# Attention block on one core: set-up rebuilt, two value buffers, two GpSimd chains and another plan

## The chip, the cores and the metric

One core of a Trainium2 chip runs the kernel. The metric is the device time in microseconds (us) of one execution, the median of several; lower is better. The engines are named as in the profile: PE (matrix multiply), ACT (ScalarE), DVE (VectorE), POOL (GpSimd) and SP (which only issues DMAs).

## The reference

```python
B, S, D, H = 1, 2048, 448, 16        # x [1,2048,448], wqkv [448,1344], wo [448,448], bf16
Dh = D // H                          # 28
qkv = (x @ wqkv).reshape(B, S, 3, H, Dh).transpose(2, 0, 3, 1, 4)
q, k, v = qkv
p = softmax(einsum("bhqd,bhkd->bhqk", q, k) * Dh ** -0.5)
return einsum("bhqk,bhkd->bhqd", p, v).transpose(0, 2, 1, 3).reshape(B, S, D) @ wo
```

## The kernel before

**Tiling.** The 16 heads form four groups of four; a group's heads lie in four strips of 32 partitions (28 rows of the head, one row for offsets, three of padding). Queries are cut into four blocks of 512, keys into 16 blocks of 128. A group with a query block is a *window*; there are 16. A window has 16 rows (key blocks) of four score tiles, one for each head, 128 keys by 512 queries; 1024 tiles in all. A tile is one matmul of a strip pair of KB with one of QB (L935), which leaves in PSUM the exponent of the softmax term, scaled so that its upper bits, taken as an integer, are already close to the bits of the bf16 result. The largest key entry of a head (KMAX) times |q| serves as an upper bound that is taken off; it comes in through the other strip of each pair, which holds |q| on the query side and the negative maximum on the key side.

**Three ways to finish a tile.** (1) ACT: two tiles share a double bank PA, and one Exp over 128x1024 (L1364) writes bf16 to a PTA buffer. (2) DVE and POOL: DVE makes DU (L1139) and DV (L1142), POOL multiplies them to DG (L1145), DVE adds DG and writes PTD (L1158); the tile's bank PD (three of them) is held until then. (3) POOL alone ("lone chain", `start_g`): DVE copies the bank to SG (L1071) and frees it, then POOL does six steps on it: GU, GE, GV, GU, SG, PTD (L1078 to L1101). There is one set of GU, GV, GE, so one such chain is in work at a time; `ahead` picks tiles some rows ahead of need.

**After that.** A row of four finished tiles is multiplied with V (VA) into the one bank PO (L1203), which adds up 16 rows; a window's sum goes to OSB, its reciprocal denominators travel through DRAM and come back broadcast as RRB, POOL multiplies (L1038) to OT, and PE multiplies OT with `wo`. The first two windows (NF = 2) first do only their first four rows (FB = 4) each, with a provisional bound from key block 0 alone (KPART[:, 0]); `task_factor` later computes the factor that brings those sums to the final bound.

**Set-up.** x comes in blocks of 512 rows: XS[0] to XS[2] by plain loads on SP and the fourth transposed by DMA (L310). WK is loaded on ACT's queue (L299), WQ behind XS[0] on SP (L306). PE transposes a block in two halves of eight 128x112 pieces (L462) into PSUM; DVE or ACT copies to XT (L473, L475). POOL spreads WK's columns to the 32-row strips (WKP, L425), ACT does the same for WQ (L426). Four matmuls make K of block 0 (L578), four make Q (L714). ACT writes Q twice (QB, L730 and L732), DVE takes absolute values (QP, L738), reduces K to its largest entries (L587, L592), and |q| times that bound goes to the other strips, by DVE (L749) or POOL (L746). ACT copies K with a mask and a bias (`bndcol`, L596 and L599). The maxima of all key blocks (`task_kmax`, L630) become NK, which DMAs replicate into the key strips (L652). Constants are filled by memsets: the unit rows of XT (L359) and V's ones (L360) on DVE, the masks `mcol`, `bdiff`, `selcol`, `bndcol` on POOL (L348 to L356).

**Order.** Nothing is left to a run-time scheduler. At build time the kernel simulates its engines with fixed costs: each `Op` has an engine, a cost, a latency, dependencies, a priority and conditions. `try_pe`, `try_act` and `try_static` pick the next operation whenever an engine is free, and the instructions are issued in the order found. `pos` counts score tiles started. The lists in PLAN hold 16 numbers, one for each window: from which row lone chains are taken (AHEAD), how long POOL holds back for DVE's tiles (GCLEAR), by how much a PE operation may overrun the end of a running exponential (SLK, in `fits`), due times of Q, K, V and so on. Engines run their own queues in order, so an instruction that waits holds everything behind it on that engine. An operation of kind "sb" (fast SBUF-to-SBUF on DVE, L762 and L766) is started only near the end of a POOL instruction.

Of the kernel before, what the change touches and what calls it, by code (L numbers as in the profile page):

```python
# [21 lines left out]
P = 128  # L22
H = 16
HP = 32
G = 4
# [7 lines left out]
KEPS = 1e-6  # L33
# [12 lines left out]
    "PVROWS": [8, 10, 10, 3, 6, 7, 11, 7, 7, -10, 7, 7, 11, 11, 11, 9],  # L46
    "AHEAD": [16, 9, 16, 15, 7, 10, 12, 8, 12, 13, 11, 6, 13, 7, 11, 5],
    "GCLEAR": [0.4, -0.4, -0.3, 0.3, 0.2, 0.7, 0.3, -0.1, 0.2, 1, 0.5, 1, 0.4, 0.8, 1.4, 0.1],
    "SCLEAR": [0, 1.1, 1.8, 1.7, 1.4, 0.4, 0.7, 0, 0.3, 1.5, 0.1, 0.9, 1.8, 2, 0.4, 1.8],
    "LEAD1": [39, 10, 29, 7, 3, 3, 6, 33, 3, 26, -6, 23, -9, -3, 11, 13],  # L50
    "LEAD2": [35, 8, 37, 43, 45, 13, 27, 43, 38, 19, 20, 49, 27, 32, 24, 29],
    "LEAD3": [0.1, 13, 2, 7, 45, 0.1, 8, -6, 5, -9, 24, 2, -2, 27, 12, 1],
    "LEADC": [30, 0, 39, 26, 16, 30, 14, 14, 37, -2, 23, 43, 34, 20, -3, 13],
    "PVMORE": [3, 9, 6, 1, 2, 5, 3, 4, 4, 3, 2, 6, 2, 2, 0, 8],
    "QFROM": [8, 0, 13, -18, 2, -7, -14, -3, -29, 0, 15, -30, 2, 27, 2, 20],
    "QBY": [64, 33, 84, 35, 80, 63, 48, 35, 70, 68, 37, 26, 24, 83, 73, 82],
    "QLEAD": [-88, 27, 38, -61, -3, -56, 48, 32, 6, -83, 0, 17, 28, -85, -90, 11],
    "KFROM": [34, 11, 29, -12, -10, -8, 19, 19, 18, 30, 41, -14, 27, 26, 8, 2],
    "KBY": [23, 12, 48, -4, 29, 50, 40, 54, 30, -2, 2, 49, 14, 48, 9, 40],
    "KLEAD": [34, 27, -74, -63, -7, -50, 32, 24, 1, -25, -43, -62, 18, -27, -8, 47],  # L60
    "VFROM": [-2, 8, 7, 30, -2, 49, 8, 15, 40, -1, -5, 24, 46, -9, 35, 43],
    "VBY": [41, 25, 52, 0, 56, 14, 11, 57, 57, 37, 59, 4, 57, -8, 17, 49],
    "VLEAD": [48, 73, 0, -21, 9, -23, 6, 54, 46, 20, 21, -27, -34, 9, -21, -1],
    "NORM": [20, 10, -10, 38, 6, 40, 20, 10, -14, -4, 9, -10, -18, 20, 32, -1],
    "TAIL": [8, 8, 40, 1],
    "PART": [-34, -19, 34, 37, -30, 40, 3, 30],
    "OUT": [0, 10, 28, 39, 20, -22, 7, -6, 5, -8, -2, 39, -30, -10, 13, 39],
    "SLK": [0.2, 0.22, 0.21, 0.19, 0.12, 0.21, 0.2, 0.12, 0.24, 0.11, 0.08, 0.22, 0.17, 0.19, 0.27, 0.12],
# [6 lines left out]
TDEP = 0.12  # L75
# [12 lines left out]
EVU = 0.598  # L88
DISS = 0.6
# [28 lines left out]
def kernel(  # L118
# [29 lines left out]
    NG = 3  # L148
    GMAX = 1
# [42 lines left out]
    FE2 = 80  # L192
# [3 lines left out]
    TE = 0  # L196
    CPE = 1
    REDP = 0
    TW = 0
    XLAT = (4.6, 7.3, 8.9, 9.6)  # L200
    WQLAT = 5.9
    XSP = 1
    KP0 = -4377
    KP1 = -4375
    KP2 = -4485
    BP2 = 34
    PBND = ((3,), (2, 3))
    VE = 16
    UV = 4
    BW = (-1, 4, 1)  # L210
    THF = (0, 1, 0, 0)
    EVP = (-1200, -4365, -700, 0)
    KEVP = (0, 200, 200, 200)
    WQE = 'ACT'
    QORD = 0
    KCH = ((1, 2), (2, 4))
    RCH = ((1, 4), (0, 1))
    XT3 = 14.0
    XBAR = True
    KENG = ('ACT', 'DVE', 'DVE', 'DVE')  # L220
    HENG = ('ACT', 'DVE', 'DVE', 'DVE')
# [24 lines left out]
    RK0 = sb([P, 1], F32, "RK0")  # L246
# [3 lines left out]
    VA = [sb([P, NKT, HG, HP], BF16, f"VA{g}") for g in range(G)]  # L250
# [8 lines left out]
    GU = sb([P, QW], F16, "GU")  # L259
    GV = sb([P, QW], F16, "GV")  # L260
    GE = sb([P, QW], F32, "GE")
# [24 lines left out]
    maskm = sb([P, QW], BF16, "maskm")  # L286
# [3 lines left out]
    bndcol = [sb([P, 1], F32, f"bndcol{pr}") for pr in range(2)]  # L290
    mcol = sb([P, 1], F32, "mcol")
    bdiff = sb([P, 1], F32, "bdiff")
    negm = sb([P, NF, HP], BF16, "negm")
# [5 lines left out]
    nc.scalar.dma_start(out=WK[:, :, 0:GW], in_=wq3[:, :, D:D + GW])  # L299
    for b in range(NQC):  # L300
        if b < NQC - 1:
            nc.sync.dma_start(out=XS[b][:], in_=x_perm[:, b * TPC:(b + 1) * TPC, :])
        elif not XBAR:
            nc.sync.dma_start(out=XS[b][:], in_=x2[0:QW].rearrange("(t p) c -> p t c", t=TPC))
        if b == 0:
            nc.sync.dma_start(out=WQ[:, :, 0:GW], in_=wq3[:, :, 0:GW])  # L306
# [19 lines left out]
    for i in range(HG):  # L326
        nc.gpsimd.affine_select(out=onescol[:], in_=onescol[:], compare_op=ALU.not_equal, fill=1.0,
                                base=-(HP * i + Dh), pattern=[[0, 1]], channel_multiplier=1)
    for g in range(G):
# [4 lines left out]
    UB = 96  # L334
# [13 lines left out]
    nc.gpsimd.tensor_scalar(out=mcol[:], in0=onescol[:], scalar1=MARG, scalar2=-MARG, op0=ALU.mult, op1=ALU.add)  # L348
    nc.gpsimd.tensor_tensor(out=bdiff[:], in0=onescol[:], in1=mcol[:], op=ALU.subtract)
    for pr in range(2):  # L350
        nc.gpsimd.memset(selcol[pr][:], 0.0)
        for st in range(HG):
            if st % 2 == pr:
                nc.gpsimd.memset(selcol[pr][HP * st:HP * (st + 1), :], 1.0)
        nc.gpsimd.tensor_tensor(out=bndcol[pr][:], in0=bdiff[:], in1=selcol[pr][:], op=ALU.mult)
        nc.gpsimd.tensor_tensor(out=bndcol[pr][:], in0=bndcol[pr][:], in1=mcol[:], op=ALU.add)  # L356
    nc.scalar.copy(out=WO[:], in_=zrow[:, None, 0:D].to_broadcast([P, G, D]))
    for b in range(NQC - 1):
        nc.vector.memset(XT[b][1][UB:CK + 2, 1, :], 1.0)  # L359
# [1188 lines left out]
```

## Time and profile before

| | us |
|---|---|
| median of 3 runs (406.26 to 406.28) | 406.28 |
| the profiled execution: span from first to last instruction | 404.5 |
| first exponential starts (timeline) | 11.87 |
| last exponential ends (timeline) | 396.90 |
| DVE's first softmax tile starts (timeline, L1139) | 25.11 |

The profiled execution is one other execution than the timed ones; its page gives its span and no separate time, so the 1.8 us between span and median are start and end outside the instructions. A group's row reads: line, engine, operation, what it writes <- reads, shapes, how often | busy us, mean ns of one | idle time of the engine just before, and what ended it. Instructions of one engine overlap a little, so a mean can exceed the pace: 1165 ns for an exponential that comes every 0.918 us. Busy time of DVE is 387.5 us, of POOL 345.0, of PE 353.5.

### The profile page before, as it was taken

The page shows a single profiled execution, that of the slowest core. Times are in us where ns is not written, and L with a number is a line of the kernel's source. Part 1 is how long each engine was busy: PE and PEld are TensorE (multiplying, and loading weights), DVE is VectorE, ACT ScalarE, POOL GpSimd, SP SyncE. Part 2 cuts the span into 40 slices and gives each one's busy share as a digit, 9 for nine tenths or more (in the row PEclk, how much of TensorE's full clock was granted, in tenths as well). Part 3 has the DMA queues.
Part 4 walks back from the last instruction along what each step waited for, and adds up shares of the span by engine and source line. Part 5 has one row for each costly group of instructions (what it writes and reads, how often), then busy time and mean ns, then how long its engine had stood idle before and what let it go on. Part 6 is the DMA issues. An engine that isn't in the chain of part 4 may idle for free.

```text
span 404.5 us, 7615 instructions
## 1 busy us (share of the span) xinstructions
PE 353.5 (87%) x2596; PEld 115.6 (29%) x2607; DVE 387.5 (96%) x700; ACT 393.5 (97%) x432; POOL 345.0 (85%) x370
## 2 busy tenths in 40 slices
PE   7999979998898888899888987888898898989896
PEld 4342332322232232322322232222223322222232
DVE  6989999999999999999999999999999999999995
ACT  5999999999999999999999999999999999999994
POOL 3429999879899889899999899988899997989990
PEclk9999999999999999999999999999999999999999
DMA  9351120212301020110411000010220002001012
GB/s 212 51 85 42 47 55 26 36 44 40 68 2 47 0 53 7 18 41 2 101 39 33 24 20 10 1 48 1 71 56 16 32 2 56 11 26 51 5 69 91
DMA packets 36446, 16.58 MB, mean 41 GB/s; under 512 B 28784, under 2 KB 33136, under 8 KB 36408
## 3 DMA queue, kind: packets, MB, share of 16 engines
q1 hardware_dynamic: 35800, 15.89, 16.8%
q8 instruction: 20, 0.33, 0.3%
q10 hardware_dynamic: 608, 0.22, 0.2%
q14 instruction: 18, 0.15, 0.1%
HBM read 7.44 MB, written 1.97 MB: 23 GB/s over the span
## 4 chain that ended last, share of the span: by engine, by line
ACT 42%; DVE 23%; PE 15%; POOL 10%; issue 7%; DMA 1%; SPq 0%; DVEq 0%; POOLq 0%
ACT PTA L1364 42%; PE PA L935 6%; DVE PTD L1158 6%; DVE DU L1139 5%; DVE DV L1142 5%; POOL DG L1145 5%; PE PO L1203 4%; PE PD L935 2%; POOL GU L1086 1%; POOL SG L1088 1%; PE PO L714 1%; DMA QB<-QP 1%; DVE SG L1071 1%; POOL OSB L1011 1%; POOL PTD L1101 1%
## 5 line engine op out<-in xcount | busy, mean ns | idle before, releaser
L1364 ACT ACTIVATE PTA<-PA 128x1024 bf16<-128x1024 f32 x419 | 384.5, 1165 | 0.8 <-PE PA L935 0.6
L935 PE MATMUL PA<-QB,KB 64*128 64x512 bf16 x837 | 168.5, 381 | 39.5 <-ACT PTA L1364 36.0
L1145 POOL TENSOR_TENSOR DG<-DV,DU 128x512 f16<-128x512 f16 x162 | 185.1, 1154 | 16.8 <-DVE DV L1142 11.9
L935 PEld LDWEIGHTS <-KB 64*128 64x128 bf16 x1024 | 61.5, 93 | 181.7 <-issue 173.6
L1158 DVE SCALAR_TENSOR_TENSOR PTD<-PD,DG 128x512 uint16<-128x512 f32 x162 | 109.0, 679 | 3.1 <-POOL DG L1145 2.0
L1142 DVE SCALAR_TENSOR_TENSOR DV<-PD,DU 128x512 f16<-128x512 uint16 x162 | 107.9, 680 | 0.8
L1139 DVE TENSOR_SCALAR DU<-PD 128x512 f16<-128x512 uint16 x162 | 106.8, 677 | 1.9 <-PE PD L935 1.7
L1203 PE MATMUL PO<-PTA,VA 128*32 128x512 bf16 x837 | 83.1, 385 | 0.1
L935 PE MATMUL PD<-QB,KB 64*128 64x512 bf16 x187 | 68.6, 377 | 3.5 <-DVE PTD L1158 2.0
L1203 PE MATMUL PO<-PTD,VA 128*32 128x512 bf16 x187 | 53.6, 386 | 0.0
L1203 PEld LDWEIGHTS <-VA 128*32 128x32 bf16 x1024 | 18.8, 94 | 46.5 <-issue 44.9
L1086 POOL TENSOR_TENSOR GU<-GV,GU 128x512 f16<-128x512 f16 x25 | 28.9, 1154 | 2.2 <-DVE QP L762 1.5
L1088 POOL TENSOR_TENSOR SG<-SG,GU 128x512 f32<-128x512 f32 x25 | 28.9, 1155 | 1.9 <-DVE QP L762 0.8
L1084 POOL TENSOR_TENSOR GV<-GE,GU 128x512 f16<-128x512 f32 x25 | 28.9, 1156 | 1.7 <-DVE QP L762 0.8
L1038 POOL TENSOR_TENSOR OT<-OSB,RRB 128x512 bf16<-128x512 f32 x15 | 19.0, 1270 | 1.5 <-DVE PTD L1158 1.5
L1078 POOL TENSOR_SCALAR GU<-SG 128x512 f16<-128x512 uint16 x25 | 15.4, 617 | 5.1 <-DVE SG L1071 3.4
L1071 DVE COPY SG<-PD 128x512 f32<-128x512 f32 x25 | 17.0, 681 | 0.5 <-PE PD L935 0.3
L714 PE MATMUL PO<-XT,WQP 112*128 112x512 bf16 (+1 forms) x52 | 16.9, 385 | 0.3 <-DVE OSB L1023 0.3
L1081 POOL TENSOR_SCALAR GE<-SG 128x512 f32<-128x512 uint16 x25 | 15.4, 617 | 2.0
L578 PE MATMUL PO<-XT,WKP 112*128 112x512 bf16 (+1 forms) x52 | 16.9, 385 | 0.1
L794 PEld LDWEIGHTS <-XT 112*128 112x128 bf16 x256 | 13.6, 98 | 10.7 <-issue 10.4
L1101 POOL TENSOR_SCALAR PTD<-SG 128x512 uint16<-128x512 f32 x25 | 15.5, 618 | 0.9
(120 smaller groups left out, 197.4 us busy)
## 6 DMA issues: line engine op xcount, KB each, us to landing
RRB<-SCR SPq DMA_DIRECT2D x15, 256.0 KB
QB<-QP SPq DMA_DIRECT2D x56, 32.0 KB
KB<-NK SPq DMA_DIRECT2D x12, 128.0 KB
XS<-in_x_dram SPq DMA_DIRECT2D x3, 448.0 KB
QB<-QB SPq DMA_DIRECT2D x28, 32.0 KB
out_dram<-XS SPq DMA_DIRECT2D x2, 448.0 KB
KB<-KB SPq DMA_DIRECT2D x6, 128.0 KB
RRB<-SCRF SPq DMA_DIRECT2D x2, 256.0 KB
```

Source lines behind the costliest of these rows:

```text
L714: ops = chain_mm(CC, lambda cc: nc.tensor.matmul(out=ap(), lhsT=WQP[g][0:rows_of(g, c, cc), cc, :], rhs=XT[c][cc // 2][0:rows_of(g, c, cc) ...
L935: nc.tensor.matmul(out=ap, lhsT=KB[g % 2][i // 2][a:a + 64, j * P:(j + 1) * P], rhs=QB[w % NQB][i // 2][a:a + 64, :], start=True, stop=Tru ...
L1071: cp = add(Op("DVE", CPY, lambda: nc.vector.tensor_copy(out=X[:], in_=PX[slot.idx][:]), deps=[sop], prio=n - PLAN["LEADC"][now()], lat=0.165))
L1084: g3 = add(Op("POOL", PTT, lambda: nc.gpsimd.tensor_tensor(out=GV[:], in0=GE[:], in1=GU[:], op=ALU.mult), deps=[g2], prio=prio + 2, kind=" ...
L1086: g4 = add(Op("POOL", PTT, lambda: nc.gpsimd.tensor_tensor(out=GU[:], in0=GV[:], in1=GU[:], op=ALU.mult), deps=[g3], prio=prio + 3, kind=" ...
L1088: g5 = add(Op("POOL", PST, lambda: nc.gpsimd.tensor_tensor(out=X[:], in0=X[:], in1=GU[:], op=ALU.add), deps=[g4], prio=prio + 4, kind="g", ...
L1139: p1 = add(Op("DVE", P1, lambda: nc.vector.tensor_scalar(out=DU[b][:], in0=lo, scalar1=SIG / 65536, scalar2=SIG * (SS - 0.5), op0=ALU.mult ...
L1142: p2 = add(Op("DVE", P1, lambda: nc.vector.scalar_tensor_tensor(out=DV[b][:], in0=lo, scalar=65536 * (SS - 0.5 + CE / C3), in1=DU[b][:], o ...
L1145: gq = add(Op("POOL", PTT, lambda: nc.gpsimd.tensor_tensor(out=DG[b][:], in0=DV[b][:], in1=DU[b][:], op=ALU.mult), deps=[p2], prio=n, kind ...
L1158: f = add(Op("DVE", P1, lambda: nc.vector.scalar_tensor_tensor(out=PTD[st["s"].idx][:].bitcast(U16), in0=PX[slot.idx][:], scalar=EBITS + C ...
L1203: nc.tensor.matmul(out=PO[HP * st:HP * (st + 1), :], lhsT=VA[g][:, j, st, :], rhs=r["p"][i][1](), start=first, stop=last, tile_position=(0 ...
L1364: nc.scalar.activation(out=PTA[pslot.idx][:, 0:len(ns) * QW], in_=PA[s.idx][:, 0:len(ns) * QW], func=ACT.Exp, bias=ACT_BIAS, scale=ACT_SCALE)
```

## The change

- *Loads*: WK moves from ACT's queue to SP's, behind XS[0] and ahead of WQ.
- *x block 0 in quarters*: four groups of four transposes, each with its own bank and copy (DVE, ACT, DVE, DVE); each of K's and Q's matmuls waits only for its quarter. All copies of blocks 1 and 2 are on DVE.
- *Weights*: WKP of group 0 in two halves on POOL; WQP of group 0 on POOL behind them (was ACT).
- *Memsets*: XT's unit rows and V's ones move from DVE to POOL, with 32-bit writes of two bf16 ones; only two VA buffers are filled.
- *Bounds*: the key maxima no longer multiply |q|. The query strips get plain |q| (ACT's Abs for the first, DVE's sign clear for the others); the key side gets the maxima as the bias of a masked copy (`masked_evac`): for key block 0 on DVE, with the bias made by four one-column products, and likewise for key block 1, with the final maximum. RK0, KEPS, bdiff and the product of |q| with KPART in group 0 go. NK is DMA-replicated for blocks 2 and 3 first and for 0 later, no more for 1. `cut0` takes `negm` from KB.
- *Tile order* in the first two provisional windows: heads 0 and 1 of all four rows, then heads 2 and 3.
- *Values*: VA has two buffers, used as g % 2; V of groups 2 and 3 waits until the rows two groups back are used.
- *POOL chains*: two sets of GU, GV, GE and four SG; up to two lone chains are open (GMAX = 2), their steps interleaved; a step is not started within 0.117 us of the one it needs.
- *Planner*: lists kept sorted, `fits` computed once per call, and all PLAN lists new.

```diff
@@ PLAN (a few of the lists)
-    "GCLEAR": [0.4, -0.4, -0.3, 0.3, 0.2, 0.7, 0.3, -0.1, 0.2, 1, 0.5, 1, 0.4, 0.8, 1.4, 0.1],
+    "GCLEAR": [13.61, -5, -25.21, -13.97, -1.69, -13.36, 6.76, -0.38, -3.2, -3.12, -2.48, -17.3, 3.29, -13.88, -8.82, -4.93],
-    "SLK": [0.2, 0.22, 0.21, 0.19, 0.12, 0.21, 0.2, 0.12, 0.24, 0.11, 0.08, 0.22, 0.17, 0.19, 0.27, 0.12],
+    "SLK": [0.15, 1.26, 0, 1.5, 0.26, 1, 0.1, 0.2, 1.85, 2.96, 0, 1.41, 3.4, 0.18, 0.27, 0.31],
...
-    NG = 3
-    GMAX = 1
+    NG = 4
+    NCH = 2
+    GMAX = 2
+    XE = ('DVE', 'ACT', 'DVE', 'DVE')
-    VA = [sb([P, NKT, HG, HP], BF16, f"VA{g}") for g in range(G)]
+    VA = [sb([P, NKT, HG, HP], BF16, f"VA{g}") for g in range(2)]
-    nc.scalar.dma_start(out=WK[:, :, 0:GW], in_=wq3[:, :, D:D + GW])
...
         if b == 0:
+            nc.sync.dma_start(out=WK[:, :, 0:GW], in_=wq3[:, :, D:D + GW])
             nc.sync.dma_start(out=WQ[:, :, 0:GW], in_=wq3[:, :, 0:GW])
...
+    nc.gpsimd.memset(XT[0][1][UB:CK + 2, 1, :].bitcast(F32), ONES2)
...
+        nc.gpsimd.tensor_tensor(out=bndcol[0][pr][:], in0=onescol[:], in1=selcol[pr][:], op=ALU.mult)
-    nc.gpsimd.tensor_tensor(out=bdiff[:], in0=onescol[:], in1=mcol[:], op=ALU.subtract)
...
-    for b in range(NQC - 1):
-        nc.vector.memset(XT[b][1][UB:CK + 2, 1, :], 1.0)
-    nc.vector.memset(VA[0][:].rearrange("p j h e -> p (j h) e")[:, :, Dh:HP], 1.0)
...
+    for cc in range(CC):
+        tv = xbank[cc].bitcast(BF16)
+        def tr0(cc=cc, tv=tv):
+            for t in range(TPC):
+                nc.tensor.transpose(out=tv[0:CK, t * P:(t + 1) * P], in_=XS[0][:, t, cc * CK:(cc + 1) * CK], identity=ident[:])
+        def ev0(cc=cc, tv=tv):
+            o, i = XT[0][cc // 2][0:CK, cc % 2, :], tv[0:CK, 0:QW]
+            if XE[cc] == "DVE":
+                nc.vector.tensor_copy(out=o, in_=i)
+            else:
+                nc.scalar.copy(out=o, in_=i)
...
+    def masked_evac(k, sc, ap, dep, kmax, pb, p0, p1):
+        bcs = []
+        for i in range(HG):
+            st = SI[i]
+            eng = nc.gpsimd if k else nc.vector
+            bcs.append(add(Op("POOL" if k else "DVE", 0.21, lambda st=st, eng=eng: eng.tensor_scalar(
+                out=bndcol[k][st % 2][HP * (st ^ 1):HP * ((st ^ 1) + 1), :], in0=kmax[HP * st:HP * (st + 1), :],
+                scalar1=mcol[HP * st:HP * (st + 1), 0:1], scalar2=0.0, op0=ALU.mult, op1=ALU.add), deps=dep,
...
+        return [add(Op("DVE", EVB, lambda pr=pr: nc.vector.tensor_scalar(
+            out=KB[0][pr][:, sc * QW:(sc + 1) * QW], in0=ap(), scalar1=selcol[pr][:, 0:1], scalar2=bndcol[k][pr][:, 0:1], op0=ALU.mult, op1=ALU.add),
+            deps=bcs[2 * pr:2 * pr + 2], prio=p1 if pr else p0)) for pr in range(2)]
...
+            e0 = add(Op("ACT", 0.62, lambda: nc.scalar.activation(
+                out=QB[0][0][:], in_=ap, func=ACT.Identity, bias=offscol[:, 0:1], scale=YSC),
...
+            ab = add(Op("ACT", 0.62, lambda: nc.scalar.activation(
+                out=QB[0][0][HP:2 * HP, :], in_=ap[0:HP, :], func=ACT.Abs, scale=YSC),
...
+            e1 = add(Op("DVE", EVK, lambda: nc.vector.tensor_scalar(
+                out=QB[0][1][:], in0=ap, scalar1=YSC, scalar2=offscol[:, 0:1], op0=ALU.mult, op1=ALU.add),
...
+            for i in range(1, HG):
+                o = add(Op("DVE", TS3, lambda i=i, st=st: nc.vector.tensor_scalar(
+                    out=QB[0][i // 2][HP * (st ^ 1):HP * ((st ^ 1) + 1), :].bitcast(U16), in0=QB[0][i // 2][HP * st:HP * (st + 1), :].bitcast(U16),
+                    scalar1=0x7FFF, scalar2=None, op0=ALU.bitwise_and), deps=[e1 if i > 1 else e0],
...
     def tile_of(n):
-        k, i = divmod(n, HG)
-        w, j = row_of(k)
+        if n < NF * FB * HG:
+            w, m = divmod(n, FB * HG)
+            j, i = m // 2 % FB, m // (2 * FB) * 2 + m % 2
+        else:
+            k, i = divmod(n, HG)
+            w, j = row_of(k)
...
     def start_g(n, sop, slot, sg):
+        ch = g_seq[0] % NCH
         g_seq[0] += 1
+        U, V, E = GU[ch], GV[ch], GE[ch]
...
-            deps=[cp] + g_prev, prio=prio, kind="g", elig=quiet, lat=0.0))
+            deps=[cp] + g_prev[ch], prio=prio, kind="h", elig=quiet, lat=0.0))
```

## The prediction

> **What bounds the kernel now.** I read the page's busy shares first, then the costliest groups, then the timeline of both ends, then the chain of waits of the first 14 us, then the busy time by stretch.
>
> ```profile
> span 404.5 us, 7615 instructions
> ...
> PE 353.5 (87%) x2596; PEld 115.6 (29%) x2607; DVE 387.5 (96%) x700; ACT 393.5 (97%) x432; POOL 345.0 (85%) x370
> ...
> L1364 ACT ACTIVATE PTA<-PA 128x1024 bf16<-128x1024 f32 x419 | 384.5, 1165 | 0.8 <-PE PA L935 0.6
> ...
> L1145 POOL TENSOR_TENSOR DG<-DV,DU 128x512 f16<-128x512 f16 x162 | 185.1, 1154 | 16.8 <-DVE DV L1142 11.9
> ```
>
> ACT's exponentials run back to back: 419 of them, 384.5 us, 0.8 us idle ahead of them. The timeline has the first at 11.87 and the end of the last at 389.65 + 7.25 = 396.90; the 7.6 us behind are the tail. So the time is: start of the first exponential, plus the exponentials ACT has to do at 384.5 / 419 = 0.918 us, plus tail. 837 of the 1024 score tiles go to ACT, 162 to DVE with POOL (L1139, L1142, L1145, L1158), 25 to POOL alone (L1078 to L1101). Time falls if ACT starts sooner or if the other two take more tiles.
>
> ```profile
> 4.56 1.57 DVE L359 MEMSET XT<- 18x512 bf16 x3
> ...
> 4.64 0.88 PE L462 MATMUL PD<-ident,XS 128*112 128x128 bf16 x12 [0.17 <-DMA XS<-in_x_dram]
> ...
> 6.42 0.63 DVE L473 COPY XT<-PD 112x1024 bf16<-112x1024 bf16 x1
> ...
> 11.87 8.46 ACT L1364 ACTIVATE PTA<-PA 128x1024 bf16<-128x1024 f32 x9 [0.62 <-PE PA L935]
> ```
>
> The transposes of the first x block are in PSUM by about 5.5, but DVE, busy with memsets, fetches them at 6.42. The chain of waits before the first exponential (start, length, what):
>
> ```profile
> 6.50 0.56 DVE XT L473
> ...
> 8.55 0.45 PE PD L578 x2
> 9.02 0.69 DVE KPART L587
> 9.71 0.20 DVE QP L738
> 9.91 0.07 DVE KPART L592
> 10.01 0.34 DVE QB L749
> 10.39 1.02 DVE QB L749
> ```
>
> The second L749 takes 1.02 where the first took 0.34; POOL's L746 runs from 10.15 to 11.26, and it ends when that does.
>
> ```profile
> 0.00:12.00 12.00, 8.85 (x67) 4.95 (x67) 8.83 (x45) 6.81 (x9) 5.53 (x27) 1.00 0.98 210
> 12.00:40.00 28.00, 26.27 (x191) 9.31 (x190) 25.37 (x46) 27.90 (x31) 14.70 (x23) 1.00 0.29 49
> 40.00:80.00 40.00, 35.50 (x286) 12.43 (x284) 39.01 (x69) 39.88 (x45) 37.62 (x38) 1.00 0.18 39
> ```
>
> Columns: length, then busy time of PE, weight loads, DVE, ACT, POOL. From 40 to 397 the nine stretches sum to 350.1 us of DVE and 324.8 of POOL in 357: DVE is full too, POOL has 32 us left.
>
> **Set-up, to the first exponential.** Times on the profile's clock; what no row shows is an estimate from the row named.
> x lands. WK's load on ACT's queue took 7.9% of the 16 DMA engines over the first 6 us, 0.47 us, while XS[0] was moving. Behind XS[0] it frees that much: transposes at 4.2 in place of 4.64 (bounds 4.1, and 4.64 if WK was not in the way).
> Transposes and copies. Twelve transposes took 0.88 us, so 0.055 each and 0.22 of depth; the first quarter is ready at 4.62. DVE copies a quarter in 0.41 (112x512 row of L473), ACT in 0.58 (L475). DVE takes the first, third and fourth, done by 5.85. DVE is free for it: L359 and L360 (1.5 and 0.27) move to POOL, and maskm shrinks to a quarter (L346 and L347 were 0.49 and 0.35).
> K. WK lands after x, about 4.8; its pad copy (L425, 0.56) becomes two halves, done by 5.4. POOL is free: its memsets moved ahead of it (L359's for block 0, one row of 0.5 us) replace bdiff and four small products of 0.2 (L349, L355, L356). The last K matmul starts at 5.9 and ends at 6.3; before, 8.39 + 0.59 = 8.98. Q's four follow at 0.22 and end at 7.2, its pad copy (0.56, now on POOL behind K's) being done by 6.0.
> The two ways into the first score pair. DVE: reduction 0.69 (L587), two one-column products of 0.15 (L592), masked copy of K with scale and bias 0.74 (L726 is the nearest row), so 8.2; then one sign clear over 32 partitions, 0.36 (the free L749), 8.55. ACT: two evacuations, 0.69 each at 0.59 steps (L730, L732), 8.45. The 1.02 of L749 has no successor, as POOL's L746 is gone.
> Score pair to exponential: 11.46 to 11.87, 0.41. That makes 8.95. Some eleven hand-overs between engines at 0.04, about what the listed rows leave between them, give **9.4**, 2.45 sooner. Bounds: 8.9 with none lost, 10.2 with x no sooner and one DVE copy held 0.35 by a POOL op.
>
> **Does the gain survive behind it?** DVE now makes the second Q and K copies (0.74 each), two more sign clears and two products: 2.3 us that ACT and POOL did. What hides them is the new order of the first 32 tiles: exponentials 1 to 4 need heads 0 and 1 only, 4 x 0.918 = 3.7 us of cover. Without it ACT would stall about 2.3. Exponential 9 needs block 1's Q, 7.3 us after the first, at 16.7: DVE does the 2.3 us, four x copies of 0.65, and Q1's evacuation, copy and four clears (0.69 + 0.28 + 4 x 0.28), ending near 16: 0.7 to spare. Exponential 17, due at 24.1, needs K of block 1: before, this waited for a DMA of the maxima (issued 21.48, POOL's FW still waiting for it at 26.05, with exponential 17 due at 26.6); now two masked copies of 0.74 stand there, about 21.6. SP issues WK (0.42) ahead of WQ, XS[1], XS[2], WV and the transposing load, so each goes out 0.42 later; the last one's issue ended at 10.54 and its K matmuls ran at 18.18, which covers it. POOL's pads and zeros end near 8, far ahead of FW at 24.7.
>
> DVE's first softmax tile was at 25.11. Moved work adds 2.1 us net on DVE (2.3 and 0.8 for masked copies, less L749's 1.39 against four clears of 0.28, L738, L766 and L594), some of it into the 1.4 us it waited for Q at 24.10: its start moves by -0.8 (bounds -2, +0.5).
>
> **The sum for starts.** ACT does 2.18 tiles a us, DVE and POOL 187 tiles in 371 us, 0.50. Moving ACT by -2.4 and DVE by -0.8 moves the end by (2.18 x 2.4 + 0.50 x 0.8) / 2.68 = 2.1 us (bounds 1.3 and 2.7).
>
> **Two chains on POOL.** One lone tile costs POOL 3 x 1.155 + 3 x 0.617 = 5.3 us and DVE one copy of 0.6 (its pace; L1071), a third of a DVE tile; per extra chain POOL pays 4.9 net and 0.67 tile is won. Interleaving fills the gaps between dependent steps (189.12, 189.82, 190.53 in the timeline: steps of 0.70 for 0.62 of work) and lets one wait while the other runs. If half of the 32 us goes that way: 3.2 chains, 2.2 tiles, 0.8 us. Bounds 0 and 1.4. I take the middle, the idle being spread in small pieces. Two value buffers only hold V of groups 2 and 3 until the group two back has been used; V is made a group ahead and DVE, not V, is scarce: nothing, and if it did come late, PV's 24 tile buffers stand between it and ACT.
>
> **The plan's other numbers** I take at zero with bounds of -2 and +2: exponentials run at 0.918 where the fast stretches show 0.905 ((7.50 - 1.165) / 7 at 298.97), so 5 us of small lateness can be lost or gained. The tail keeps its 7.6.
>
> Sum: 404.5 - 2.1 - 0.8 = 401.6 for the span. The 1.8 us between the span and the median of the runs (406.28) I carry over: **403.4 us**.
>
> [...]
> [...]
>
> **Rivals.**
> [...]
> B. More: K and Q at their bounds and three quarters of POOL's idle time won, some lateness of exponentials removed: 2.7 + 1.2 + 1.6 gives 400.8. For it: 5 us of lateness exist. Against: DVE is at 98% from 40 on, so extra tiles need POOL alone.
> C. Slower: PE late for ACT. The allowance by which PE may overrun an exponential's end (SLK) goes from 0.08-0.27 to 1.0-3.4 in seven of the 16 windows, 7 x 26 = 183 exponentials. The chain shows only 0.06 to 0.20 us of "issue" between an exponential and its release near 301 us; one group of four PV matmuls is 0.23 (0.62 for eight, less 0.39). A group ahead of the score pair costs about 0.13. If one in four meets it, 0.03 on average, ACT loses 5.5 us, the end 5.5 x 0.81 = 4.5: 407.9. It decides above 2.9 / 0.81 / 183 = 0.02 us each. Against: PE is idle 39.5 us ahead of score pairs, 36.0 of it waiting for ACT.
> D. The change does not do what it says: Abs needs its own table, two loads of 1.28 (L316's row) ahead of the first exponential: 403.4 + 0.81 x 2.6 = 405.5.
>
> **Chances.** Forecast 0.54, A 0.11, B 0.13, C 0.19, D 0.03. The measurement of this kernel tells 0.2% (0.8 us) from no change. C is slower but for a tenth, A and D lie near the edge: faster 0.74, same 0.08, slower 0.18. Range 400.5 to 406.5; it leaves out most of C and a little of B. The forecast's own range is 402.0 to 404.8, from the bounds of starts and chains.
>
> **What would show it.** First exponential at 9.4 in the timeline (8.9 to 10.2), the transposes at 4.2, last K matmul by 6.5; no idle time ahead of L1364 at exponentials 5, 9 and 17; 27 to 30 lone POOL chains and some 826 to 832 tiles on ACT; DVE's sign clears at 0.3. Wrong would be: mean step of exponentials over 0.93 (C), 0.6 us and more on DVE's 16-bit copies (A), two table loads (D), or a first exponential after 10.5.

## The result, and the profile after

The changed kernel takes 406.75 us in the median (406.19 to 408.77), the kernel before on the same chip 406.27 (406.25 to 406.33). The ratio is 1.002, 95% interval 1.0011 to 1.003: no gain, and rather 0.5 us slower. The forecast of 403.4 and its range up to 406.5 were wrong. Note the spread as well: 2.6 us where the kernel before has 0.08.

The page of the profiled execution (406.57 us), parts 1, 4 and 5:

```profile
span 404.8 us, 7598 instructions
...
PE 355.7 (88%) x2604; PEld 113.2 (28%) x2604; DVE 389.5 (96%) x705; ACT 392.0 (97%) x427; POOL 360.9 (89%) x400
...
DVE 46%; POOL 27%; ACT 12%; issue 6%; PE 6%; DMA 2%; SPq 1%; DVEq 0%; ACTq 0%; POOLq 0%
...
L1369 ACT ACTIVATE PTA<-PA 128x1024 bf16<-128x1024 f32 x417 | 384.8, 1091 | 2.9 <-PE PA L938 2.2
...
L1147 POOL TENSOR_TENSOR DG<-DV,DU 128x512 f16<-128x512 f16 x162 | 184.9, 1154 | 9.8 <-DVE DV L1144 8.7
...
L938 PE MATMUL PD<-QB,KB 64*128 64x512 bf16 x191 | 70.7, 376 | 11.6 <-DVE PTD L1160 7.6
```

The same two rows of the kernel before, the chain's shares by engine and the PD tiles:

```profile
ACT 42%; DVE 23%; PE 15%; POOL 10%; issue 7%; DMA 1%; SPq 0%; DVEq 0%; POOLq 0%
...
L935 PE MATMUL PD<-QB,KB 64*128 64x512 bf16 x187 | 68.6, 377 | 3.5 <-DVE PTD L1158 2.0
```

The chain's shares are the first thing to read. Before, ACT held 42%; now DVE and POOL hold 73% and ACT 12%. ACT no longer sets the end: it waits, 2.9 us ahead of its exponentials against 0.8. POOL is busy for 360.9 us instead of 345.0 and idle ahead of DG for 9.8 instead of 16.8.

Both ends of ACT's row of exponentials, from the timeline after:

```profile
9.94 7.44 ACT L1369 ACTIVATE PTA<-PA 128x1024 bf16<-128x1024 f32 x8 [0.68 <-PE PA L938]
18.21 12.94 ACT L1369 ACTIVATE PTA<-PA 128x1024 bf16<-128x1024 f32 x14 [0.84 <-PE PA L938]
...
379.22 18.10 ACT L1369 ACTIVATE PTA<-PA 128x1024 bf16<-128x1024 f32 x20
```

ACT starts at 9.94 instead of 11.87 and has 417 exponentials instead of 419 to do. The last one ends at 379.22 + 18.10 = 397.32; it was 396.90. So from first start to last end one exponential takes 387.38 / 417 = 0.929 us where it took 385.03 / 419 = 0.919. The account: -1.93 (start), -2 x 0.919 = -1.84 (two fewer), +417 x 0.0101 = +4.2 (lateness), sum +0.42. The gains came and were given back, and the question is where the 4.2 us come from. Half of them can be seen as waiting: ACT's idle time ahead of exponentials grows from 0.8 to 2.9 us. The other half is in its busy time, 384.8 / 417 = 0.923 us each against 384.5 / 419 = 0.918: exponentials that start late overlap less with the one before (mean overlap 0.163 us instead of 0.246, mean length 1091 ns instead of 1165, at the slower pace of 0.929). 0.84 us of the idle time are one stall, ahead of exponential 9. The rest has no place of its own, as the busy time by stretch shows, after and then before (ACT is the fourth pair, POOL the fifth):

```profile
80.00:120.00 40.00, 35.79 (x284) 10.66 (x282) 39.47 (x69) 39.80 (x44) 39.51 (x42) 1.00 0.14 35
200.00:240.00 40.00, 35.31 (x259) 10.79 (x251) 39.67 (x69) 39.76 (x44) 39.07 (x40) 1.00 0.07 18
280.00:320.00 40.00, 34.81 (x254) 11.14 (x252) 38.92 (x70) 39.44 (x43) 37.34 (x38) 1.00 0.09 26
```

```profile
80.00:120.00 40.00, 34.83 (x267) 10.24 (x267) 39.55 (x69) 40.00 (x45) 35.20 (x37) 1.00 0.19 42
200.00:240.00 40.00, 35.87 (x270) 11.24 (x269) 39.73 (x70) 40.00 (x45) 37.14 (x37) 1.00 0.13 30
280.00:320.00 40.00, 35.10 (x250) 12.36 (x248) 39.62 (x71) 40.00 (x45) 35.43 (x37) 1.00 0.19 45
```

In these three stretches ACT is full before and loses 0.2 to 0.6 us after, while POOL is at 37.3 to 39.5 of 40 us: little is left there to catch up with.

**A measure for this.** The kernel fixes its order by a simulation at build time. I subtract that plan's start of each DVE instruction from the traced start and take the median around a moment. If the plan's costs are right, the difference stays constant. Plan ends are the kernel's own, too: 397.95 before, 395.32 after, 2.6 us sooner.

```
distance to the plan (us) at     40    120    200    280    360    385   growth
before                          1.14   1.23   1.21   1.18   1.20   1.21    0.07
after                           0.82   1.86   2.53   3.52   4.37   4.40    3.58
```

The kernel before runs to plan. The changed one falls behind evenly from end to end, by 3.6 us.

**What POOL does that the plan does not know.** Two pieces of POOL's timeline, after and before:

```profile
301.30 0.62 POOL L1106 TENSOR_SCALAR PTD<-SG 128x512 uint16<-128x512 f32 x1
302.00 1.20 POOL L1083 TENSOR_SCALAR GU<-SG 128x512 f16<-128x512 uint16 x2
```

```profile
302.48 0.62 POOL L1101 TENSOR_SCALAR PTD<-SG 128x512 uint16<-128x512 f32 x1
303.17 0.62 POOL L1078 TENSOR_SCALAR GU<-SG 128x512 f16<-128x512 uint16 x1
```

Two GU in a row take 1.20, so the second starts 1.20 - 0.62 = 0.58 after the first. But from a PTD to the GU behind it 0.70 pass (301.30 to 302.00; 302.48 to 303.17 before): 0.115 more. Over the whole trace after, a GU starts late by this in 25 cases of 29, a GE in 19 (2.4 us in all), a PTD in 7 (0.9 us); GV, GU and SG of the tensor-tensor kind in one each. The kernel before charged 0.12 to every GU and GE and to each step that directly follows the one it needs. The changed planner keeps a step 0.117 us away from the one it needs, but otherwise charges 0.115 to the GU alone, whatever stands ahead. So the late GE and PTD, 3.3 us of POOL, are missing from the plan (less some 0.3 for the three GU that are charged and on time), and the plan fills POOL to the brim on top. That is about the size of the 3.6 us. POOL's order is fixed (in the trace after its steps start in the order of issue), so each lateness goes on: POOL's DG to DVE's PTD, which holds its PD bank (PE's idle time ahead of PD tiles that PTD ends: 2.0 us before, 7.6 after), and PE's queue holds the next pair for ACT behind that PD tile.

So my theory became: the plan undercounts POOL's steps, and a full POOL passes it to ACT. The rivals: C of the prediction (the new SLK lets PE come late), and the set-up alone.

### The profile page after: what moved, and what is told of

It is laid out like the page before. It is cut to its first block, busy times and chain, and to the rows that moved or that the text cites. A ratio compares the mean times of both kernels' runs of the same rounds, so it can differ in the third digit from the quotient of the medians.

```text
span 404.8 us, 7598 instructions
## 1 busy us (share of the span) xinstructions
PE 355.7 (88%) x2604; PEld 113.2 (28%) x2604; DVE 389.5 (96%) x705; ACT 392.0 (97%) x427; POOL 360.9 (89%) x400
## 4 chain that ended last, share of the span: by engine, by line
DVE 46%; POOL 27%; ACT 12%; issue 6%; PE 6%; DMA 2%; SPq 1%; DVEq 0%; ACTq 0%; POOLq 0%
POOL DG L1147 13%; DVE PTD L1160 13%; DVE DU L1141 12%; ACT PTA L1369 11%; DVE DV L1144 11%; POOL SG L1093 3%; POOL GV L1089 3%; POOL GU L1091 2%; DVE SG L1076 2%; POOL PTD L1106 2%; POOL GE L1086 2%; PE PA L938 2%; POOL OT L1041 2%; POOL GU L1083 1%; DVE KB L613 1%
## 5 line engine op out<-in xcount | busy, mean ns | idle before, releaser
L1369 ACT ACTIVATE PTA<-PA 128x1024 bf16<-128x1024 f32 x417 | 384.8, 1091 | 2.9 <-PE PA L938 2.2
L938 PE MATMUL PA<-QB,KB 64*128 64x512 bf16 x833 | 170.9, 382 | 26.0 <-ACT PTA L1369 23.0
L938 PEld LDWEIGHTS <-KB 64*128 64x128 bf16 x1024 | 57.1, 93 | 171.9 <-issue 162.2
L1091 POOL TENSOR_TENSOR GU<-GV,GU 128x512 f16<-128x512 f16 x29 | 33.4, 1154 | 2.9 <-DVE QP L765 2.8
L1089 POOL TENSOR_TENSOR GV<-GE,GU 128x512 f16<-128x512 f32 x29 | 33.5, 1157 | 0.7 <-DVE QP L765 0.6
L1093 POOL TENSOR_TENSOR SG<-SG,GU 128x512 f32<-128x512 f32 x29 | 33.5, 1157 | 0.4 <-DVE QP L765 0.3
L1076 DVE COPY SG<-PD 128x512 f32<-128x512 f32 x29 | 19.8, 681 | 0.6 <-POOL DG L1147 0.5
L1083 POOL TENSOR_SCALAR GU<-SG 128x512 f16<-128x512 uint16 x29 | 17.8, 617 | 2.3 <-DVE QP L765 0.3
L794 PE MATMUL PO<-WV,XT 112*128 112x112 bf16 x240 | 17.7, 213 | 1.7 <-DVE OSB L1026 0.8
L1086 POOL TENSOR_SCALAR GE<-SG 128x512 f32<-128x512 uint16 x29 | 17.8, 618 | 1.6
L1106 POOL TENSOR_SCALAR PTD<-SG 128x512 uint16<-128x512 f32 x29 | 17.9, 620 | 1.3 <-PE PA L938 0.6
```

The source lines that it names most:

```text
L794: nc.tensor.matmul(out=ap()[:, jj * GW:(jj + 1) * GW], lhsT=XT[jq][cc // 2][0:CK, cc % 2, jj * P:(jj + 1) * P], rhs=WV[:, cc, g * GW:(g + ...
L938: nc.tensor.matmul(out=ap, lhsT=KB[g % 2][i // 2][a:a + 64, j * P:(j + 1) * P], rhs=QB[w % NQB][i // 2][a:a + 64, :], start=True, stop=Tru ...
L1076: cp = add(Op("DVE", CPY, lambda: nc.vector.tensor_copy(out=X[:], in_=PX[slot.idx][:]), deps=[sop], prio=n - PLAN["LEADC"][now()], lat=0.165))
L1089: g3 = add(Op("POOL", PTT, lambda: nc.gpsimd.tensor_tensor(out=V[:], in0=E[:], in1=U[:], op=ALU.mult), deps=[g1, g2], prio=prio + 2, kind= ...
L1091: g4 = add(Op("POOL", PTT, lambda: nc.gpsimd.tensor_tensor(out=U[:], in0=V[:], in1=U[:], op=ALU.mult), deps=[g3], prio=prio + 3, kind="h", ...
L1093: g5 = add(Op("POOL", PST, lambda: nc.gpsimd.tensor_tensor(out=X[:], in0=X[:], in1=U[:], op=ALU.add), deps=[g4], prio=prio + 4, kind="h", ...
```

## The experiments

All medians in us, with the lowest and highest run; ratios against the kernel before on the same chip, and the growth of the distance to the plan from 40 to 385 us:

```
run            median (lowest-highest)    ratio [95%]                growth
after          406.75 (406.19-408.77)     1.002  [1.0011, 1.003]      3.58
e_half         403.49 (403.41-403.69)     0.9921 [0.9906, 0.9936]     0.35
e_contig       407.68 (406.59-408.89)     1.0023 [1.0009, 1.0038]     3.70
e_plus         407.81 (407.40-409.66)     1.0035 [1.0021, 1.0049]     4.77
warm8          406.81 (406.50-407.69)     1.0007 [0.9998, 1.0016]     3.92
before_half    406.26 (406.25-406.27)     0.9996 [0.9987, 1.0005]      0.06
no_fill        411.22 (410.65-411.44)     1.0116 [1.0103, 1.0129]     8.66
two_chains     406.45 (406.20-408.25)     1.0012 [1.0001, 1.0024]     1.36
one_chain      405.46 (405.32-407.16)     0.9987 [0.9975, 0.9998]     0.09
before_search  406.87 (406.85-407.75)     1.0016 [1.0008, 1.0025]     0.17
one_chain_b    405.83 (405.45-407.64)     0.9994 [0.9985, 1.0004]     0.21
one_chain_c    405.37 (405.29-406.74)     0.9982 [0.9974, 0.9991]     0.18
one_chain_w8   405.72 (405.21-406.10)     0.9985 [0.9976, 0.9994]     0.12
```

The kernel before takes 406.60 us on the chip of e_half, e_contig, e_plus and warm8, and 406.27 to 406.29 on the others, so runs of different chips are better compared by their ratios.

**Less POOL work, same order (e_half).** GE over half of its columns takes 404 ns instead of 618, so the 29 chains free 6.2 us of POOL; order, SLK and all lists stay. The other half of GE is filled with ones once, near the start.

```diff
-            out=E[:], in0=lo, scalar1=1.0, ...
+            out=E[:, 0:QW // 2], in0=lo[:, 0:QW // 2], scalar1=1.0, ...
```

> The changed kernel, GE computed for half of its 512 columns only (the rest holds a constant); same order. Theory (POOL's pace): each GE is shorter by about 0.2 us, 29 times, so POOL gains 6 us, is no longer late, and the time falls to 403 to 404. Rival (PE late by SLK): 406.5 +- 0.5.

Page of this run:

```profile
span 401.9 us, 7600 instructions
...
ACT 51%; DVE 26%; PE 13%; issue 6%; DMA 2%; POOL 1%; SPq 1%; DVEq 0%
...
L1371 ACT ACTIVATE PTA<-PA 128x1024 bf16<-128x1024 f32 x417 | 382.9, 1134 | 1.7 <-PE PA L940 1.5
...
L940 PE MATMUL PD<-QB,KB 64*128 64x512 bf16 x191 | 70.0, 376 | 6.4 <-DVE PTD L1162 3.2
```

The time falls by 3.3 us, to 403.49, and is 3.1 us below the kernel before on the same chip. (That it lands near the forecast of 403.4 is chance: this kernel leaves work out.) POOL's share of the chain goes from 27% to 1%, ACT is back at 51%, the distance to the plan grows by only 0.35 us and PE's wait for PTD falls from 7.6 to 3.2 us. SLK and the order are those of the changed kernel, so C cannot be what cost these 3.3 us.

**The same cut in the kernel before (before_half).** A control: if a lighter POOL helps any such kernel, e_half shows nothing of the change.

```diff
-            out=GE[:], in0=lo, scalar1=1.0, ...
+            out=GE[:, 0:QW // 2], in0=lo[:, 0:QW // 2], scalar1=1.0, ...
```

> The kernel before with GE of its lone chains computed for half of the columns (the rest a constant); order as before. Theory (POOL was on time in the kernel before, and late only in the changed one): nothing to win, 406.3 +- 0.3. Rival (POOL set the pace there too): 3 us less, as in e_half.

406.26 against 406.27: POOL was no limit before. The change made it one.

**More POOL work (e_plus).** A memset of one column ahead of each GE.

```diff
+            nc.gpsimd.memset(PADT[:], 0.0)
+            return nc.gpsimd.tensor_scalar(out=E[:], in0=lo, ...
```

> The changed kernel with one small POOL memset (128x1, about 0.1 us) ahead of each GE, 29 in all; the rest in the same order. Theory (POOL's pace sets the end): 29 x 0.1 = 3 us more, 409 to 410. Rival (PE late by SLK): POOL has 10% idle time and takes it up, 406.5 to 407.

The median, 407.81, lies between the two expectations, and the growth rises from 3.58 to 4.77 us. The direction is right, and the trace explains the size: behind the same neighbours a GE starts only some 0.04 us later with the memset than without (0.62 us instead of 0.58 behind a PTD, 0.74 instead of 0.70 behind a GU). 29 x 0.04 = 1.2 us, which is the rise of the growth: in this range what POOL gets more to do arrives at the end in full.

**The width of what GE reads (e_contig).** I suspected that the late start of GE comes from its reading every second 16-bit word of SG.

```diff
-            out=E[:], in0=lo, scalar1=1.0, ...
+            out=E[:], in0=X[:], scalar1=1.0, ...
```

> The changed kernel with one edit: step GE of the lone POOL chains reads SG as whole 32-bit words instead of the lower 16 bits of each (the value of GE is then another one); the order of all instructions stays. Theory (POOL's real pace is slower than the plan's by about 0.115 us at each GE, 29 times, and DVE, PE and ACT fall behind with it): if the wider read takes the extra 0.115 us away, some 3 us of POOL go, the mean step of the exponentials falls from 0.930 towards 0.921 and the time to about 403.5 to 404.5. Rival (PE itself is late, because SLK lets other matmuls in ahead of score pairs): same order, same lateness, 406.5 +- 0.5. If GE keeps its extra time, nothing moves and the run tells nothing.

GE starts just as late behind the same neighbours: POOL's idle time ahead of its 29 GE is 1.6 us in both profiles, and one takes 617 ns here and 618 after. The stride is not the reason, and the run tells nothing of the theory (its median, 407.68, is carried up by five of ten runs above 408, which the last experiments are about).

What sorts the late steps from the others can be read in the trace after, though. It is not the step just ahead but the last tensor-scalar step that POOL ran, with any tensor-tensor steps between. If that was a GU, all 19 GE and all 6 PTD come about 0.115 us late and all 3 GU on time; if it was a GE or a PTD, all 25 GU come late, and all 10 GE and 18 of 19 PTD on time. e_contig sorts in the same way, and so does e_plus, with its memset between. GE and PTD multiply by 1.0 and GU by another factor, but they differ in their types too, and no run changes one of these alone; what within POOL costs the 0.115 stays open.

**Right costs in the plan (two_chains, one_chain).** The planner charges 0.115 to a GU or GE whose neighbour ahead on POOL is of another kind (not to a GE behind a PTD), and the PLAN lists are searched again for it, once with two chains and once, for one_chain alone, with GMAX = 1.

```diff
-        g1 = add(Op("POOL", PTS + 0.115, lambda: ...
+        g1 = add(Op("POOL", PTS, lambda: ...
...
+                        if step_j == 0 and pool_j[0] != 0 or step_j == 1 and pool_j[0] not in (1, 5):
+                            o.dur += 0.115
...
-    GMAX = 2
+    GMAX = 1
```

> The changed kernel with POOL's costs in the plan mended (0.115 us more for GE too, and for GU and GE only where the step before them is of another kind) and PLAN lists searched anew for these costs; two chains as in the change. By its own plan the last operation ends 1.8 us later than the changed kernel's plan said and 0.8 us earlier than the plan of the kernel before. Theory (the changed kernel lost its gain because POOL's real pace was slower than planned): the chip now follows the plan within about 1 us to the end, the mean step of the exponentials is 0.920, time 405.3 to 406.0. [...]

> As two_chains, but one lone chain open at a time (GMAX = 1) and lists searched for that: the new set-up without the interleaving. By its plan it ends 0.6 us earlier than the kernel before. Theory: set-up alone gives what is left, 405.4 to 406.1, and two chains are worth no more than 0.3 us. Rival (the chains are what the change gains by, and the new set-up nothing): 406.3 or more, and two_chains well below it.

The plans end at 397.12 and 397.31: with right costs the second chain is worth 0.2 us on paper. On the chip two_chains still falls behind by 1.36 us (its PTD steps start late in 10 cases, 1.3 us, which this cost rule still does not charge). So most of the slip of 3.58 us goes with the right costs, but the median, 406.45, lies above its expectation of 405.3 to 406.0. one_chain runs to plan and meets its expectation. Chains by engine of two_chains, then of one_chain:

```profile
DVE 40%; ACT 22%; POOL 21%; PE 8%; issue 7%; DMA 1%; SPq 0%; DVEq 0%; ACTq 0%; POOLq 0%
```

```profile
ACT 50%; DVE 16%; PE 15%; POOL 8%; issue 7%; DMA 3%; DVEq 0%; POOLq 0%; ACTq 0%
```

one_chain has as many exponentials as the kernel before (419), starts at 9.89 and is some 0.8 us faster: with the new set-up and one chain a gain is left.

**Is it the set-up, or the search of the lists?** before_search is the kernel before with only the numbers in its PLAN lists searched anew in the same way, no other line changed; one_chain_b is one_chain unchanged; one_chain_c has lists searched further (plan end 397.06).

> The kernel before with only its PLAN lists searched anew under its own costs (a control for one_chain, whose lists were searched too). Its own plan ends at 397.5 instead of 397.95; the chip kept a constant distance to that plan in the kernel before (1.1 to 1.2 us from 40 us to the end). If the gain of one_chain came from the search of the lists and not from the new set-up, this kernel gains the same 0.8 us: 405.4 to 405.6. If the set-up is what gains, this one gains at most the 0.4 us by which its plan ends sooner: 405.8 to 406.3.

> one_chain again, unchanged, beside the control above on the same chip: theory (the new set-up brings some 0.8 us once the plan's POOL costs are right) 405.3 to 405.7 in the median, ratio 0.997 to 0.999. If the earlier figure was scatter, 406 and more.

> one_chain with its PLAN lists searched further: its plan ends at 397.06 instead of 397.31, and the chip kept 8.1 us from that plan's end to the median of its runs in one_chain and 8.3 in the kernel before: 405.0 to 405.4, ratio 0.997 to 0.998, with the chip's distance to the plan flat from 40 us to the end (0.5 to 0.8). If the plan is too tight for the chip, the distance grows by over 0.5 us and the time stays at 405.5 or above.

before_search misses both of its expectations: this search makes the kernel before 0.6 us slower, though its planned end came sooner (397.18 in the plan of the kernel as it ran, not the 397.5 expected). Its last exponential is planned 0.4 later and ends 0.5 later on the chip. So a search alone does not bring one_chain's gain. one_chain's last exponential is planned only 0.1 us sooner than before and ends 0.7 us sooner: most of its gain is that it stays 0.6 us behind its plan where the kernel before stays 1.2 behind, a difference that is there at the first exponential already. That speaks for the set-up; but one_chain keeps the new tile order, the two value buffers and a changed cost rule too, and no run separates these. one_chain_b, at 405.83, misses its expectation and does not repeat the gain beyond its interval; one_chain_c, at 405.37, meets its own and does. Why the same kernel gives 405.5 once and 407.5 another time is the next question.

**Do PE's fillers cost ACT time? (no_fill)** The kernel fills PE's free time with matmuls on zeros (L1318 to L1330); here they are left out after 20 us.

```diff
-        if o.fn is None:
+        if o.fn is None or o.kind == "K" and o.start > 20:
```

> The changed kernel without the filler matmuls of PE after the set-up (zeros, added to nothing); the rest in the same order. Theory (PE is late because it waits in its queue for banks that DVE and POOL free late): no change, 406.5 +- 0.7. Rival (PE itself is short of time and lets score pairs wait): 37 x 0.2 to 0.4 us less work on PE, exponentials closer to 0.92, 404 to 405.5.

Windows of this run (granted clock is the last number but two):

```profile
40.00:80.00 40.00, 35.69 (x283) 11.72 (x281) 39.41 (x70) 39.96 (x44) 37.74 (x39) 1.00 0.21 47
80.00:120.00 40.00, 35.90 (x274) 10.23 (x273) 38.63 (x66) 38.80 (x42) 39.47 (x41) 0.93 0.15 35
200.00:240.00 40.00, 35.99 (x224) 9.08 (x222) 36.70 (x63) 36.85 (x40) 36.19 (x37) 0.79 0.06 18
```

Both expectations fell, and the run decides nothing about lateness, because something else happened: without the fillers the granted clock drops to 0.93 (80 to 120) and 0.79 (200 to 240) where the changed kernel has 1.00 in both stretches, PE gets 224 matmuls done from 200 to 240 where it did 259 and ACT 40 instructions where it did 44, and 4.5 us are lost in the median. In these two profiles the fillers go with a clock that stays at 1.00.

**PE's rate in the set-up (warm8, one_chain_w8).** In the profile after, the first transposes come at 0.107 us each, not 0.055:

```profile
2.92 1.06 PE L427 MATMUL PA<-zrow,zeros 128*128 128x512 bf16 x2
4.37 1.46 PE L439 MATMUL PD<-ident,XS 128*112 128x128 bf16 x12 [0.39 <-DMA XS<-in_x_dram]
...
5.88 1.16 PE L582 MATMUL PD<-XT,WKP 112*128 112x512 bf16 x4
```

Twelve take 1.46 us where they took 0.88. The change has six warm-up matmuls ahead of them; the trace before shows eight. I first thought that two more would restore the rate in time:

```diff
-        add(Op("PE", 2 * MM, lambda: warm(n), ...
+        add(Op("PE", 2 * MM, lambda n=n: [warm(n) for _ in range(3 if n == 5 else 1)], ...
```

> The changed kernel with eight warm-up matmuls as in the kernel before, in place of six; order otherwise the same. In the changed kernel the first transposes ran at 311 ns and their weight loads at 213, in the kernel before at 219 and 130. Theory (PE is slow because it was idle or not busy long enough ahead of the transposes): transposes at 219 ns, first exponential 0.3 to 0.6 earlier than 9.94 and the time up to as much less, 406.0 to 406.5, since DVE's part of the set-up moves too. Rival (the slow transposes come from the loads or from the four banks): still 311 ns.

The transposes were as slow as before and the median did not move: the expectation fell. What I overlooked is in the runs' spread: highest 407.69, where 7 of the 20 runs of the changed kernel lie at 407.72 to 408.77. The profile of one_chain_b fell on such a run (407.52 us):

```profile
4.59 1.53 PE L439 MATMUL PD<-ident,XS 128*112 128x128 bf16 x12 [0.62 <-POOL XT L497]
...
6.34 1.91 PE L582 MATMUL PD<-XT,WKP 112*128 112x512 bf16 x4
8.05 1.91 PE L703 MATMUL PD<-XT,WQP 112*128 112x512 bf16 x4
...
10.72 0.59 ACT L709 ACTIVATE QB<-PD 32x512 bf16<-32x512 f32 x1
```

Here K's and Q's matmuls come at (8.05 - 6.34) / 4 = 0.43 us, all of them at half rate, where the profile after has 0.22 to 0.25. Abs ends at 11.3 instead of 9.26, the first exponential starts at 11.80, and the distance to the plan is 2.6 us from 40 us on and never grows: the 2 us between two runs of one kernel lie in the first 12 us. PE stood idle for 0.4 us (after) and 0.6 us (one_chain_b) between its sixth warm-up and the transposes. Eight warm-ups close that pause. So the last run was one_chain_c with warm8's edit:

> one_chain_c with eight warm-up matmuls in place of six, so that PE is busy without a pause from 1.26 to the first transpose at 4.6 (with six it stands idle for 0.4 to 0.6 us before it). Theory: the runs of the changed kernels that lie 1.5 us and more above the fastest (7 of 20 of the changed kernel, 7 of 32 of the three with one chain by 1.2 us and more) are those in which PE's set-up matmuls ran at half rate to the end (634 ns each, first exponential at 11.80 in the profile of one_chain_b with its 407.52), because the pause fell into the stretch by which PE's rate is set; without the pause these runs go: no run above 406.5, highest within 1.0 us of the lowest, median 405.3 to 405.7. Rival: the late change of rate has to do with chance alone and not with the pause: two of some eleven runs at 406.6 to 407.6 as before.

No run is above 406.10, and highest and lowest are 0.9 us apart, as expected; the median, 405.72, lies just past its expectation. (Of the 32 runs with one chain and six warm-ups, five and not seven lie 1.2 us and more above their lowest: 406.91, 407.16, 407.52, 407.64, 406.74.) With that rate none in 11 happens by chance about once in six; warm8's ten runs also stay within 1.2 us, where the changed kernel has 7 of 20 at 1.5 to 2.6 above its lowest and, on warm8's own chip, e_contig and e_plus with six warm-ups have 8 of 20 at about 1.5 and more. The profiles point the same way: in all five with eight warm-ups, old set-up or new, PE has changed its rate by 5.9 us; of the nine with six, four change later (6.6 in e_half, 7.0 in e_contig, 8.7 in e_plus, 10.4 in one_chain_b). I take the pause as likely, not as shown, and no run shows a stretch by which PE's rate is set. The price is in the median, 405.72 against 405.37: in its timeline the transposes can't start before the eighth warm-up is done, at 4.66, where they start at 4.49 in one_chain_c, and the first exponential comes at 10.25 instead of 9.83.

When the rate changes differs from profile to profile: PE is busy from 1.26, with the pause named above where there are six warm-ups, and changes at 4.0, 4.8 and 5.7 in three profiles with the old set-up, at 5.5 after, at 6.6 in e_half and at 10.4 in one_chain_b. What sets the moment is not shown. The column of the granted clock reads 1.00 all the while (to 12 us before and after, to 8 us in e_half, e_contig, e_plus and warm8); the spacing and the lengths of matmuls show the change, that column does not.

## Why the prediction was wrong, step by step

**What bounds the kernel, and the sum for starts: right in kind, too large in size.** ACT started 1.93 sooner where I had 2.47 (9.4); 9.94 lies inside the bounds of 8.9 to 10.2. In one_chain, which keeps the set-up and runs to plan, 0.8 us of it reach the end (0.5 in one_chain_b), where the step had 2.1; where the rest stays is not shown. DVE's first softmax tile moved by -1.35 (25.11 to 23.76) instead of -0.8.

**The set-up's pieces.** "Twelve transposes took 0.88 us, so 0.055 each": they took 0.107, because this now stands on the path at a moment when PE still runs at half rate (0.107 a step up to 5.5 us, 0.056 from 5.7 on). Before, DVE's memsets held the copy until 6.42 and covered it, whatever PE did (in before_half the transposes took 1.40 without costing anything). I costed the removal of the memsets but not what they had hidden. This is only a part of the 0.54 us that the start was off: in two_chains, whose profile has these transposes 0.055 apart, the first exponential comes at 9.75. The rest: transposes began at 4.37 (4.2 predicted), K's last matmul ended near 7.04 (6.3), ACT's two evacuations, by which the chain of waits runs, ended at 9.26 (8.45); from the score pair to the exponential it was 0.64 (0.41). The sign clears took 0.28 and Abs 0.59 with no second table load, so D did not happen.

**"0.7 to spare" at exponential 9: wrong by 1.5.** The timeline after shows why:

```profile
15.92 1.91 PE L582 MATMUL PD<-XT,WKP 112*128 112x512 bf16 x8
16.37 0.29 DVE L754 COPY QB<-QB 128x512 bf16<-128x512 bf16 x1
16.70 1.23 DVE L757 TENSOR_SCALAR QB<-QB 32x512 uint16<-32x512 uint16 x4
17.75 0.11 PEld L938 LDWEIGHTS <-KB 64*128 64x128 bf16 x4 [0.42 <-DVE QB L757]
17.76 0.60 PE L938 MATMUL PA<-QB,KB 64*128 64x512 bf16 x4
```

DVE's copies and clears end at 17.93, not near 16, since Q's matmuls for block 1 are spread between score pairs (14.08 and 15.00), and eight K matmuls of 0.22 stand in PE's queue ahead of the pair until 17.7. The last wait there is for DVE's clears (0.42 on the row of the weight load). The cost is the 0.84 idle on the row of exponential 9. At 5 and 17 there is none, as predicted.

**"The plan's other numbers I take at zero", the step that failed.** The sum had -2.1 for starts, -0.8 for chains and 0 with bounds of ±2 for the rest of the plan. The rest came to +4.2 less the 0.84, so 3.4 us, and 3.6 us as slip against the plan. I looked at POOL's busy time ("POOL has 32 us left") and not at what one step costs its queue. The prediction had even listed a gap of 0.70 per step for 0.62 of work and booked it as idle time that interleaving would fill. Part of it is no idle time: in the trace after all 25 GU behind a PTD or GE and all 19 GE behind a GU cost it again, with tensor-tensor steps between or not. And filling POOL removes the slack that had kept its lateness from DVE, which e_half (-3.3 us with 6.2 us of POOL freed), e_plus (+1.2 us of slip for 1.2 us more of POOL) and before_half (0.0) show.

**Chains: the count was right, the value was not.** There are four more lone chains (29; 27 to 30 predicted) and 833 tiles on ACT (826 to 832 predicted). DVE with POOL kept its 162 tiles, where the sum had each extra chain cost a third of one, so four tiles were won and not 2.2. At the sum's 2.68 tiles a us that is 1.5 us and not 0.8; ACT's two exponentials fewer are 1.8 us of its own time. With right costs the plans with two chains and with one end 0.2 us apart, and on the chip one is 1.0 us faster in the median (405.46 and 406.45).

**Rivals.** C has its sign right (407.9) but not its mechanism: e_half keeps SLK and gets the time back. The mean step is 0.929, just below its mark of 0.93. A (0.6 us and more on DVE's 16-bit copies) is too small to matter: L765's 14 copies take 0.31 in the mean where L762's took 0.28, the longest 0.52, some 0.5 us in all, and the clears stay at 0.28. B came as 417 exponentials, and was eaten by lateness. What ended it is a rival I did not have: an engine that is planned full with costs that are about one per cent short (3.3 of 361 us).

## What to carry to other kernels

When a change fills an idle engine, price its steps start to start behind each kind of step that can stand ahead, not by their busy time: 26 late steps that the plan did not know, 3.3 us in all, go with a slip of 3.6 us here, more than the 1.8 that the extra tiles brought. A distance between the plan and the trace that grows evenly is the sign; freeing the suspected engine without touching the order is the test, together with the same cut in the kernel before. And when you shorten the path ahead of a stage, ask what the old delay covered: here a PE at half rate (K's matmuls 0.43 us apart instead of 0.22), which came with a shift of the whole run by 2 us (9.89 and 11.80 for the first exponential in two profiles of one kernel).

## What the runs showed of the hardware that was not expected

- POOL's tensor-scalar steps start about 0.115 us later (PTD to GU 0.70, GU to GU 0.58) when the last tensor-scalar step ahead of them, even with tensor-tensor steps between, was of the other sort (GU against GE and PTD): in the trace after 50 of 50 such steps are late and 31 of the 32 others on time. The stride of the input is not the reason (1.6 us of idle time ahead of GE in e_contig as in the trace after).
- PE's change from half to full rate (K's matmuls 0.43 and 0.22 us apart) came anywhere from 4.0 to 10.4 us with PE busy from 1.26; two profiles of one kernel differ by 2 us with it (first exponential at 9.89 and 11.80), and closing a pause of 0.4 to 0.6 us goes with the loss of the slowest runs (none of 11 over 0.9 us above the lowest, where 5 of 32 were at 1.2 and more).
- Without filler matmuls the granted clock fell to 0.79 between 200 and 240 us (1.00 with them), although PE's busy time is 35.99 of 40 us there (at that clock it got 224 matmuls done, where the changed kernel did 259).
